# K S and Q K from one product: Q turned and the state side by side, moved as 112 columns

## The chip, the cores and the metric

The kernel runs on one core of a Trainium2 chip. The metric is device time in microseconds (us), from the start to the end of one execution. The engines are named as in the profile: PE is TensorE (PEld its weight loads), DVE is VectorE, ACT is ScalarE, POOL is GpSimd, SP issues most of the transfers.

## What is computed

A delta-rule attention over 4 batches, 8 heads, 768 steps and a head size of 48, and behind it a feed-forward block with a SiLU gate on 3072 tokens of width 384:

```python
k_n = k / (np.linalg.norm(k, axis=-1, keepdims=True) + 1e-06)
state = np.zeros((B, H, D, D))
for t in range(S):
    kt, vt, bt = k_n[:, :, t], v[:, :, t], beta[:, :, t, None]
    y[:, :, t] = einsum('bhd,bhde->bhe', q[:, :, t], state)
    v_old = einsum('bhde,bhd->bhe', state, kt)
    state = state + bt[..., None] * einsum('bhd,bhe->bhde', kt, vt - v_old)
x = y.transpose(0, 2, 1, 3).reshape(B * S, H * D)
g = x @ w_gate
out = (g * sigmoid(g) * (x @ w_val)) @ w_out       # d_ff = 1536
```

## The kernel before

The steps are cut into 12 chunks of C = 64. Within a chunk the recurrence becomes a few matrix products for each of the 32 pairs of batch and head. With K and Q the chunk's rows and S the state at its start: K K^T gives a triangular matrix that is inverted (for two chunks at a time, a group g), R = V - K S, U = inverse times R, the output is Y = Q S + P^T U, where P is K Q^T with a mask (`mask_q`) that keeps earlier steps only, and the new state is S + K^T U. K and Q are unnormalised; norms and beta go into the inverse and into V.

Pairs are numbered by `b` and `bp` (batch = 2 b + bp) and by `j` and `par` (head = 2 j + par). A product over all of them is 32 small matmuls that each use a quarter of PE's 128x128 array: two partition halves for `par` and two output halves. `every()` runs over them in an order that goes through the four quarters. In the profile each fp32 matmul counts as two instructions, so such a product shows as x64. Six banks of PSUM matter here: `px` and `py` are pairs of banks for all attention products in turn, `ffn0` to `ffn3` belong to the feed-forward block.

`turned(c, of_q)` writes the transposed K or Q of chunk c, up to c = 2 for Q (c = 5 for K) through PE and ACT, later by one transpose on DVE (L494), from blocks that SP loads. `gram_steps` (L521) multiplies K with K or with Q; for Q two DVE operations (L539) put the masked product into `p_sb`. `advance(c)` is the chunk's chain, cut by `yield` into four steps:

1. K S into `px` (L949), Q S into `py` (L937), R = V - K S on DVE (L959).
2. U = inverse times R into `px` (L987), copied out by ACT (L1008).
3. K^T U into `px` (L1089) and added to the state on DVE (L1098); P^T U onto Q S in `py` (L1077), copied out by ACT.
4. Y is transposed (L1150) into the feed-forward block's input.

From chunk 2 on the feed-forward block of chunk c is computed while chunk c + 1 advances. `gate_val_fast` runs three rounds of ten `product4` (L1259, four matmuls of 128 columns each, eight instructions in the profile); `output_fast` runs eight products of six matmuls with 192 columns (L1465). The order of all engines is written out by hand (`manual_schedule`): at fixed places of this stream, twice in a round and twice in an output, `point` issues one step of attention work, and `fill` then issues pieces of the inverse until a budget is used up. `spent` collects what DVE time the point has cost, and is taken from that budget. A point runs the next step of `advance` if it has begun, or else a step of `prep_step`: a join of the inverse (L898, L912), the second half of a `products` generator (the K K and Q K products of an upcoming chunk), or its first half (the turning). `may_advance(c)` lets a chunk begin once its masked P exists and its inverse is joined; `finish` forces what is left. The substitution in the inverse runs on POOL (L593, L599).

What PE issues in the rounds around a chunk's first steps is thus, in the profile's order: five `product4`, a point, six `product4` with the begin of the next round, a point, and so on.

Of the kernel before, what the change touches and what calls it, by code (L numbers as in the profile page):

```python
# [20 lines left out]
def kernel(  # L21
# [25 lines left out]
    nc = tc.nc  # L47

    B, H, S, D = q.shape
    NCH = S // C  # L50
    NJ = H // 2
    NB = B // 2
# [9 lines left out]
    const = ctx.enter_context(tc.tile_pool(name="const", bufs=1))  # L62
    work = ctx.enter_context(tc.tile_pool(name="work", bufs=2))
# [10 lines left out]
    def ps_pair(name, tag):  # L74

        return pairs_of_banks[tag]
# [84 lines left out]
    def load_blocks(of_q, c):  # L161

        x, _, t = blocks_of[of_q]
        x_v = x.rearrange("b (j par) s d -> par s b j d", par=2)
        t_v = t.rearrange("p bp h d -> p (bp h d)")
        t_v = t_v.rearrange("p (b j blk d) -> p b j blk d", b=B, j=NJ, blk=C // R)
        for par in range(2):
            for at in range(0, D, R):
                m = min(R, D - at)
                rows = slice(64 * par + at, 64 * par + at + R)  # L170
                for blk in range(C // R):
                    lo = c * C + R * blk
                    nc.sync.dma_start(
                        out=t_v[rows, :, :, blk, 0:m].rearrange("p b j d -> p (b j) d"),
                        in_=x_v[par, lo : lo + R, :, :, at : at + m].rearrange(
                            "s b j d -> s (b j) d"
                        ),
                    )
# [55 lines left out]
    for n, (name, lo) in enumerate(place_of):  # L234
        m = 2 * pieces[n][4]
# [85 lines left out]
    mask_q = const.tile([128, C], FP32, name="mask_q")  # L321
    nc.gpsimd.memset(mask_q, 1.0)
    for b in range(2):
        rows = mask_q[64 * b : 64 * b + 64]
        nc.gpsimd.affine_select(
            out=rows,
# [12 lines left out]
    p_places = [const.tile([128, 1024], FP32, name=f"p_sb{i}") for i in range(2)]  # L339
    spent, late_loads = [], []  # L340
# [2 lines left out]
        if late_loads:  # L343
            late_loads.pop(0)()

    state = const.tile([128, 2, NB, NJ, D], FP32, name="state")
    kt, qt, a_sb, a_of, p_sb, xts = {}, {}, {}, {}, {}, {}

    ORDER = ((0, 0), (1, 1), (0, 1), (1, 0))
# [1 line left out]
    def half_of(x):  # L351
        return slice(64 * x, 64 * x + 64)

    def head_of(x):
        return slice(64 * x, 64 * x + D)

    def every():
        for bp in range(NB):
            for j in range(NJ):
                for n, (par, b) in enumerate(ORDER):  # L360
                    yield bp, j, par, b, bp == 0 and j == 0
# [112 lines left out]
    def banks(name, tag):  # L474

        if type(tag) is int:
            return [ps_ffn([128, 512], name, tag + i) for i in range(2)]
        p = ps_pair(name, tag)
        return [p[:, 0], p[:, 1]]

    def turned(c, of_q, tag=None):

        if tag is None:
            tag = "py" if of_q else "px"
        x = qpad[c % QB] if of_q else kn_of(c)
        if of_q:
            xt = work.tile([128, NB * NJ * 2 * C], FP32, name="qt", bufs=1)
        else:
            xt = kt_of(c)
        if c >= blocks_of[of_q][1]:  # L490
            xt_v = xt.rearrange("p (b bp j i) -> p bp j b i", bp=NB, b=2, j=NJ)
            (qt if of_q else kt)[c] = xt_v
            blocks = blocks_of[of_q][2]
            nc.vector.transpose(xt, blocks.rearrange("p bp h d -> p (bp h d)"))  # L494
            spent.append(1.8)
            if c + 1 < NCH:
                late_loads.append(lambda: load_blocks(of_q, c + 1))
            return
        xt = xt.rearrange("p (bp j b i) -> p bp j b i", bp=NB, j=NJ, b=2)
        (qt if of_q else kt)[c] = xt  # L500
        p_t = banks("p_t", tag)
        for bp in range(NB):
            for j in range(NJ):
                at = slice(128 * j, 128 * j + 128)
                nc.tensor.transpose(p_t[bp][:, at], x[:, bp, 2 * j : 2 * j + 2], ident)
            if type(tag) is int:
                nc.scalar.copy(xt[:, bp].rearrange("p j b i -> p (j b i)"), p_t[bp])
        for bp in range(NB if type(tag) is not int else 0):
            nc.scalar.copy(xt[:, bp].rearrange("p j b i -> p (j b i)"), p_t[bp])
        if of_q and c + QB < Q_BLOCKS:  # L510
            load_q(c + QB)

# [42 lines left out]
    def gram(*args):  # L555
        for _ in gram_steps(*args):
            pass
# [212 lines left out]
    def recur(p, m=D):  # L770
        p = p[:, :, 0 : NB * NJ * m]
        return p.rearrange("p x (bp j d) -> p x bp j d", bp=NB, j=NJ)
# [148 lines left out]
        yield  # L921

    p_1 = []

    def advance(c):

# [5 lines left out]
        r = vin.pop(c)  # L932
        p_y = recur(ps_pair("p_y", "py"))

        def q_of_state():
            for bp, j, par, b, first in every():
                nc.tensor.matmul(  # L937
                    p_y[half_of(b ^ par), par, bp, j],
                    qt[c][head_of(par), bp, j, b],
                    state[head_of(par), b, bp, j],  # L940
                    start=first,
                    stop=False,
                    skip_group_check=True,
                )

        if c > 0:
            p_r = recur(ps_pair("p_r", "px"))
            for bp, j, par, b, first in every():
                nc.tensor.matmul(  # L949
                    p_r[half_of(b ^ par), par, bp, j],  # L950
                    kt[c][head_of(par), bp, j, b],
                    state[head_of(par), b, bp, j],
                    start=first,
                    stop=True,
                    skip_group_check=True,
                )
            if c > 1:
                q_of_state()
            nc.vector.tensor_tensor(out=r, in0=r, in1=p_r, op=ALU.subtract)  # L959
            if c == 1:  # L960
                next(p_1[0])
            spent.append(1.4)
            yield
# [18 lines left out]
        for bp, j, par, b, first in every():  # L982
            if c == 1:
                out = p_u_of[par ^ bp][half_of(b ^ bp), par, j]
            else:
                out = p_u_of[par][half_of(b), bp, j]
# [11 lines left out]
        elif c == 1:  # L998
            flat = v0.rearrange("p par bp j d -> p (par bp j d)")
            for bank in range(2):  # L1000
                p = p_u_of[bank].rearrange("p par j d -> p par (j d)")
# [24 lines left out]
        if c < 2:  # L1026
# [3 lines left out]
            for n in range(3):  # L1030
                if c > 0:
                    u = uu if n else v0
# [543 lines left out]
    def step(kind, fn, *args):  # L1576
        key = (kind, args or (1,))
        if key not in gens:
            gens[key] = [fn(*args), 0]
        if next(gens[key][0], None) != MORE:  # L1580
            gens[key][1] += 1

    def steps(kind, *args):
        return gens.get((kind, args), (None, 0))[1]
# [4 lines left out]
    def products(k_c, q_c):  # L1589

        if k_c is not None:
            turned(k_c, False)
        if q_c is not None:
            turned(q_c, True)
        yield
        if k_c is not None:
            gram(k_c, False, None, (nc.scalar.copy, nc.scalar.copy))
            if k_c % 2 == 1:
                fills.append((k_c // 2, invert(k_c // 2)))
        if q_c is not None:  # L1600
            gram(q_c, True)
        yield

# [2 lines left out]
    going = []  # L1606
# [10 lines left out]
    def may_advance(c):  # L1617
        g = c // 2
        due = {0: 0, 1: 2 + 2 * (c % 2)}.get(g, 2)
        return steps("advance", c) > 0 or (c in p_sb and steps("join", g) >= due)  # L1620

    def k_ready():

# [9 lines left out]
    def prep_step(c):  # L1633

        for g in range(1, c // 2 + 2):
            late = g == 1 and (
                hold or steps("join", g) >= 2 and steps("advance", 2) < 4
            )
            if g in inverted and steps("join", g) < (4 if g == 1 else 2) and not late:
                step("join", join if g > 1 else join_1, *((g,) if g > 1 else ()))  # L1640
                return True
        if going:
            next(going.pop())
            return True
        k_c, q_c = None, None
        if q_of and steps("advance", q_of[0] - 1) >= 3:
            q_c = q_of.pop(0)
        elif not (c > 0 and hold and not todo and k_ready()):
            return False
        if k_ready():  # L1650
            k_c = k_of.pop(0)
        gen = products(k_c, q_c)
        next(gen)
        going.append(gen)
        return True

    def point_and_fill(c, n, fill):
# [203 lines left out]
```

## Time and profile before

| | |
|---|---|
| median of 3 runs | 693.98 us (692.44 to 696.86) |
| profiled execution | 694.63 us, span of its instructions 692.9 us |
| granted TensorE clock | 0.996 |
| PE busy | 678.4 us, 98% |
| DVE busy | 410.8 us, 59% |
| ACT busy | 262.4 us, 38% |
| POOL busy | 194.4 us, 28% |
| L1259, x_ffn with the gate weights | 128.2 us, 840 instructions |
| L1465, wo_sb with h_f | 83.4 us, 480 instructions |

The span runs from the first to the last instruction of one execution; the execution's own time has 1.7 us more around it. Busy time is the union of an engine's instructions, so instructions that overlap in PE's pipeline count once, and the mean length of a PE instruction (275 ns in the first L1259 group) is latency, not the time after which the next can start. A group row has its count behind the x, then busy time in us and the mean of one in ns, then the idle time of the engine ahead of the group and what ended it.

### The profile page before, as it was taken

What the parts mean: (1) busy time and instruction counts of PE and PEld (TensorE: products, weight loads), DVE (VectorE), ACT (ScalarE), POOL (GpSimd) and SP (SyncE); (2) the same over time, 40 slices, a digit from 0 to 9 for tenths busy, and PEclk for the clock granted to TensorE, in tenths of its full rate; (3) what the DMA queues carried; (4) which work ended last, traced back from release to release, by engine and by line L of the source; (5) the groups of instructions that cost most, each with busy time, mean ns of one, the idle gap of its engine ahead of it and who ended that gap; (6) DMA issues with size and microseconds to landing.
All of it is one profiled execution on the core that took longest, in us unless ns stands there. A gap on an engine that the chain in (4) does not pass through costs nothing.

```text
span 692.9 us, 25453 instructions
## 1 busy us (share of the span) xinstructions
PE 678.4 (98%) x11272; PEld 631.5 (91%) x11272; DVE 410.8 (59%) x857; ACT 262.4 (38%) x554; POOL 194.4 (28%) x310
## 2 busy tenths in 40 slices
PE   8799999999999999999999999999999999999997
PEld 4587888656999999999999999999999999999997
DVE  6878679897657655547446457454565344333342
ACT  3785676214442532344233244233133242142230
POOL 5110031106882128820038820328800000000000
PEclk9999999999999999999999999999999999999999
DMA  9577925017550621464432373233253221221210
GB/s 132 141 185 178 271 67 163 7 35 175 127 111 13 117 79 39 104 121 78 92 74 70 70 138 70 60 82 71 66 120 70 56 63 47 56 62 46 70 46 23
DMA packets 143853, 62.29 MB, mean 90 GB/s; under 512 B 122976, under 2 KB 126048, under 8 KB 143744
## 3 DMA queue, kind: packets, MB, share of 16 engines
q1 hardware_dynamic: 141536, 60.19, 37.9%
q8 instruction: 88, 1.44, 0.9%
q10 hardware_dynamic: 2080, 0.39, 0.4%
q0 software_dynamic: 128, 0.10, 0.1%
q14 instruction: 21, 0.17, 0.1%
HBM read 53.58 MB, written 7.08 MB: 88 GB/s over the span
## 4 chain that ended last, share of the span: by engine, by line
PE 89%; DMA 4%; ACT 2%; SPq 2%; issue 1%; DVE 1%; POOL 0%; DVEq 0%; ACTq 0%
PE ffn L1259 43%; PE ffn L1465 20%; PE ffn L1355 6%; PE ffn L1382 4%; PE p_px L987 2%; PE p_px L949 2%; PE p_py L937 2%; PE p_py L521 1%; PE p_py L1077 1%; PE p_px L1089 1%; SPq L140 1%; DMA wo_sb<-in_moe_w_gate_dram 1%; DMA h_f<-in_moe_w_gate_dram 1%; PE p_px L521 1%; PE p_py L1150 1%
## 5 line engine op out<-in xcount | busy, mean ns | idle before, releaser
L1259 PE MATMUL ffn<-x_ffn,wg_sb 128*128 128x128 f32 x840 | 128.2, 275 | 0.0
L1259 PE MATMUL ffn<-x_ffn,wv_sb 128*128 128x128 f32 x840 | 128.1, 275 | 0.0
L1259 PEld LDWEIGHTS ffn<-x_ffn,wg_sb 128*128 128x128 f32 x840 | 111.1, 192 | 0.1
L1259 PEld LDWEIGHTS ffn<-x_ffn,wv_sb 128*128 128x128 f32 x840 | 110.7, 192 | 0.0
L1294 DVE TENSOR_TENSOR h_f<-sil,ffn 128x256 f32<-128x256 f32 x120 | 50.0, 418 | 78.6 <-ACT sil L1289 76.9
L1289 ACT ACTIVATE sil<-ffn 128x256 f32<-128x256 f32 x120 | 46.2, 385 | 132.4 <-PE ffn L1259 130.7
L1465 PE MATMUL ffn<-wo_sb,h_f 128*128 128x192 f32 x480 | 83.4, 327 | 0.0
L837 POOL TENSOR_TENSOR n_b<-mb,half 128x32 f32<-128x32 f32 x5 | 30.1, 6011 | 179.7 <-DVE mb L563 179.7
L1465 PEld LDWEIGHTS ffn<-wo_sb,h_f 128*128 128x128 f32 x480 | 78.1, 190 | 0.4
L1426 DVE TENSOR_TENSOR ffn<-ffn,p_sb 128x512 f32<-128x512 f32 x58 | 40.6, 699 | 63.5 <-ACT ffn L1315 62.2
L599 POOL TENSOR_TENSOR zb<-zb,tmp 128x31 f32<-128x31 f32 (+15 forms) x124 | 73.7, 595 | 9.7
L593 POOL TENSOR_TENSOR tmp<-zb,mb 128x31 f32<-128x31 f32 (+15 forms) x124 | 66.4, 535 | 16.0 <-DVE mb L580 6.6
L1259 PE MATMUL ffn<-x_t,h_f 128*128 128x128 f32 x480 | 61.1, 280 | 0.2 <-ACT ffn L1272 0.2
L1259 PEld LDWEIGHTS ffn<-x_t,h_f 128*128 128x128 f32 x480 | 56.2, 191 | 1.4 <-ACT ffn L1272 0.4
L1426 DVE TENSOR_TENSOR o_sb<-o_sb,ffn 128x192 f32<-128x192 f32 x49 | 17.3, 352 | 62.5 <-PE ffn L1465 60.9
L1272 ACT COPY ffn<-ffn 128x512 f32<-128x512 f32 x30 | 17.1, 571 | 63.8 <-PE ffn L1259 57.4
L1465 PE MATMUL ffn<-last_k,h_f 128*128 128x192 f32 x200 | 35.9, 327 | 0.0
L1423 DVE TENSOR_TENSOR h_f<-h_f,h_f 128x256 f32<-128x256 f32 x60 | 29.9, 507 | 9.1 <-PE ffn L1465 8.1
L1355 PE MATMUL ffn<-x_ffn,wg_sb 128*128 128x256 f32 x144 | 34.4, 385 | 0.2
L1355 PE MATMUL ffn<-x_ffn,wv_sb 128*128 128x256 f32 x144 | 33.9, 383 | 0.1
L1465 PEld LDWEIGHTS ffn<-last_k,h_f 128*128 128x128 f32 x200 | 32.9, 190 | 0.0
L1355 PEld LDWEIGHTS ffn<-x_ffn,wv_sb 128*128 128x128 f32 x144 | 26.9, 190 | 4.2 <-DVE h_f L1366 0.5
(306 smaller groups left out, 1096.1 us busy)
## 6 DMA issues: line engine op xcount, KB each, us to landing
h_f<-w_s SPq DMA_DIRECT2D x60, 256.0 KB, 2.8
p_sb<-w_s SPq DMA_DIRECT2D x27, 256.0 KB, 2.7
vin<-in_v_dram SPq DMA_DIRECT2D x48, 96.0 KB, 3.4
out_dram<-o_sb SPq DMA_DIRECT2D x48, 96.0 KB, 2.2
kn<-in_k_dram SPq DMA_DIRECT2D x20, 192.0 KB, 4.4
zt<-in_moe_w_out_dram SPq DMA_DIRECT2D x6, 384.0 KB, 3.6
qpad<-in_q_dram SPq DMA_DIRECT2D x36, 64.0 KB, 3.2
w_s<-h_f SPq DMA_DIRECT2D x7, 256.0 KB, 2.9
```

The source lines that it names most:

```text
L593: engine.tensor_tensor(out=t_v, in0=zb[:, 0 : j + 1, j : j + 1].to_broadcast([128, j + 1, m]), in1=mb[:, j : j + 1, j + 1 : R].to_broadcas ...
L599: engine.tensor_tensor(out=zb[:, 0 : j + 1, j + 1 : R], in0=zb[:, 0 : j + 1, j + 1 : R], in1=t_v, op=ALU.add,)
L837: nc.gpsimd.tensor_tensor(out=n, in0=mb.rearrange("p j i -> p (j i)")[:, 0 : R * R : R + 1], in1=half, op=ALU.pow,)
L1259: nc.tensor.matmul(p[:, u], w(u), moving, start=start and u == 0, stop=True, skip_group_check=True,)
L1272: nc.scalar.copy(p_y, p_x)
L1289: nc.scalar.activation(sil[:, n].rearrange("p (i n) -> p i n", i=2), p[:, 0:2], ACTF.Silu)
L1294: nc.vector.tensor_tensor(out=h_of(c, f, j), in0=sil[:, n].rearrange("p (i n) -> p i n", i=2), in1=p[:, 2:4], op=ALU.mult,)
L1355: nc.tensor.matmul(ps[name][:, i], w_sb[:, t, (f + i) * 128 : (f + i + 1) * 128], xts[c][:, t], start=(t == 0 and i == 0), stop=(t == KT - 1),
L1382: nc.tensor.matmul(p_o, hs[c, f - f % 2][:, f % 2, bp * 128 : (bp + 1) * 128], wo_sb[:, f], start=(f == 0), stop=(f == FT - 1),)
L1423: nc.vector.tensor_tensor(out=out, in0=a, in1=b, op=ALU.subtract)
L1426: nc.vector.tensor_tensor(out=out, in0=a, in1=b, op=ALU.add)
L1465: nc.tensor.matmul(p[x, part], a(f - f % 2)[:, f % 2], b(f), start=not begun and f == 0, stop=f == FH - 1, skip_group_check=True,)
```

## The change

Q turned and the state become parts of one tile `qs`: for each of the 16 index triples (b, bp, j) 64 columns of Q turned and then 48 columns of state. The turning of Q, its transpose on DVE and the state's update write into it with a stride of 112; the reads of the state and of Q elsewhere keep their form.

From chunk 3 on (`MERGED`) the Q K product in `gram` is no longer issued. In its place the first step of `advance` multiplies K with all 112 columns, `par` 0 into `px` and `par` 1 into `py`. DVE then takes R = V - K S from the last 48 columns in two operations, one for each `par`, and the masked P from the first 64 columns in three: one for `par` 0, and two for `par` 1, whose halves have to change places. Q S is issued at the start of the second step, ahead of U. The budget notes 3.4 for the first step in place of 1.4. `products` without K work ends after the turning, and a chunk may advance once Q is turned.

In the built program this removes 288 matmuls of 5710 on PE (32 in each of 9 chunks) and the order of PE's `product4` among themselves stays as it was. The wide product stands at the end of a round or of the output in eight chunks, in the middle of a round in chunk 5. From chunk 8 on the attention's steps stand a few points earlier.

```diff
-    state = const.tile([128, 2, NB, NJ, D], FP32, name="state")
+    qs = const.tile([128, 2 * NB * NJ, C + D], FP32, name="qs")
+    qs_v = qs.rearrange("p (b bp j) m -> p b bp j m", b=2, bp=NB)
+    q_t, state = qs[:, :, 0:C], qs_v[:, :, :, :, C : C + D]
...
+        late = c >= blocks_of[of_q][1]
         if of_q:
-            xt = work.tile([128, NB * NJ * 2 * C], FP32, name="qt", bufs=1)
+            xt_v = qs_v[:, :, :, :, 0:C].rearrange("p b bp j i -> p bp j b i")
...
+        if late:
+            blocks = blocks_of[of_q][2].rearrange("p bp h d -> p (bp h d)")
+            if of_q:
+                blocks = blocks.rearrange("p (u i) -> p u i", i=C)
+            nc.vector.transpose(q_t if of_q else kt_of(c), blocks)
...
     p_1 = []
+    MERGED = 3
...
-        if c > 0:
+        if c >= MERGED:
+            both = [
+                ps_pair("p_pr", tag)[:, :, 0 : NJ * (C + D)].rearrange(
+                    "p bp (j m) -> p bp j m", j=NJ
+                )
+                for tag in ("px", "py")
+            ]
+            for bp, j, par, b, _ in every():
+                nc.tensor.matmul(
+                    both[par][half_of(b ^ par), bp, j],
+                    kt[c][head_of(par), bp, j, b],
+                    qs_v[head_of(par), b, bp, j],
+                )
+            for par in range(2):
+                nc.vector.tensor_tensor(
+                    out=r[:, par],
+                    in0=r[:, par],
+                    in1=both[par][:, :, :, C : C + D],
+                    op=ALU.subtract,
+                )
+            p_sb[c] = p_places[1].rearrange(
+                "p (x bp j i) -> p x bp j i", x=2, bp=NB, j=NJ
+            )
+            for par, to, of in ((0, slice(0, 128), slice(0, 128)), (1, half_of(0), half_of(1)), (1, half_of(1), half_of(0))):
+                nc.vector.tensor_tensor(
+                    out=p_sb[c][to, par],
+                    in0=both[par][of, :, :, 0:C],
+                    in1=mask_q[of, None, None, :].to_broadcast(
+                        [of.stop - of.start, NB, NJ, C]
+                    ),
+                    op=ALU.mult,
+                )
+            spent.append(3.4)
+            yield
+            q_of_state()
+        elif c > 0:
...
-        if q_c is not None:
+        if q_c is not None and q_c < MERGED:
             gram(q_c, True)
...
-        return steps("advance", c) > 0 or (c in p_sb and steps("join", g) >= due)
+        return steps("advance", c) > 0 or ((c in p_sb or c >= MERGED and c in qt) and steps("join", g) >= due)
...
-        going.append(gen)
+        if k_c is not None or q_c < MERGED:
+            going.append(gen)
```

More of the change, by code (lines that the diff above doesn't have):

```diff
@@ L479, in banks @@
         return [p[:, 0], p[:, 1]]
+    P_T = "p (j b i) -> p j b i"
     def turned(c, of_q, tag=None):
@@ L485, in turned @@
         x = qpad[c % QB] if of_q else kn_of(c)
+        late = c >= blocks_of[of_q][1]
         if of_q:
-            xt = work.tile([128, NB * NJ * 2 * C], FP32, name="qt", bufs=1)
-        else:
[L489 to L494, printed above, removed]
+            xt_v = qs_v[:, :, :, :, 0:C].rearrange("p b bp j i -> p bp j b i")
+        elif late:
+            xt_v = kt_of(c).rearrange("p (b bp j i) -> p bp j b i", bp=NB, b=2, j=NJ)
+        else:
+            xt_v = kt_of(c).rearrange("p (bp j b i) -> p bp j b i", bp=NB, j=NJ, b=2)
+        (qt if of_q else kt)[c] = xt_v
+        if late:
[3 more added lines that the diff above has]
+            nc.vector.transpose(q_t if of_q else kt_of(c), blocks)
             spent.append(1.8)
@@ L498, in turned @@
             return
-        xt = xt.rearrange("p (bp j b i) -> p bp j b i", bp=NB, j=NJ, b=2)
-        (qt if of_q else kt)[c] = xt
         p_t = banks("p_t", tag)
@@ L506, in turned @@
             if type(tag) is int:
-                nc.scalar.copy(xt[:, bp].rearrange("p j b i -> p (j b i)"), p_t[bp])
+                nc.scalar.copy(xt_v[:, bp], p_t[bp].rearrange(P_T, j=NJ, b=2))
         for bp in range(NB if type(tag) is not int else 0):
-            nc.scalar.copy(xt[:, bp].rearrange("p j b i -> p (j b i)"), p_t[bp])
+            nc.scalar.copy(xt_v[:, bp], p_t[bp].rearrange(P_T, j=NJ, b=2))
         if of_q and c + QB < Q_BLOCKS:
```

## The prediction

> **What bounds the kernel now.** I read the page first, its engine table and its slices, then the waits of TensorE (PE) alone, then the timeline of PE through one chunk.
>
> ```profile
> span 692.9 us, 25453 instructions
> PE 678.4 (98%) x11272; PEld 631.5 (91%) x11272; DVE 410.8 (59%) x857; ACT 262.4 (38%) x554; POOL 194.4 (28%) x310
> PE   8799999999999999999999999999999999999997
> PEclk9999999999999999999999999999999999999999
> PE 89%; DMA 4%; ACT 2%; SPq 2%; issue 1%; DVE 1%; POOL 0%; DVEq 0%; ACTq 0%
> ```
>
> PE is busy in nine tenths or more of every slice from the fourth to the last but one, at full clock, and 89% of the chain that ended last is PE. A busy PE may still be a PE at less than its peak, so the second view matters more: asked for the waits of PE from 186 us (before the first chunk that the change touches) to the end, the trace answers with its heading alone, no wait. VectorE (DVE) between 171 and 693 us is at half load (third column):
>
> ```profile
> engine line waited for: us in total, times, longest us
> ...
> 171.00:693.00 522.00, 517.68 (x8498) 508.78 (x8483) 272.35 (x521) 171.74 (x365) 159.75 (x257) 1.00 0.34 75
> ```
>
> So from chunk 3 on the time is what PE's instructions cost, one behind the other. What the change is worth is a price list of PE, provided that the other engines still deliver in time. The prices stand in the timeline (start, length, engine, line; every fp32 matmul is two instructions, so 32 matmuls are x64, and a `product4` is x8):
>
> ```profile
> 447.62 1.16 PE L1259 MATMUL ffn<-x_ffn,p_sb 128*128 128x128 f32 x8
> ...
> 453.18 1.15 PE L949 MATMUL p_px<-state,kt 48*64 48x48 f32 x64
> 454.15 1.11 PE L937 MATMUL p_py<-state,qt 48*64 48x48 f32 x64
> 455.19 2.05 PE L1259 MATMUL ffn<-x_t,h_f 128*128 128x128 f32 x16
> ...
> 459.85 1.15 PE L987 MATMUL p_px<-vin,zt 64*64 64x48 f32 x64
> 460.93 1.16 PE L1259 MATMUL ffn<-x_ffn,p_sb 128*128 128x128 f32 x8
> ...
> 466.49 0.94 PE L1089 MATMUL p_px<-uu,kn 64*48 64x48 f32 x64
> 467.24 1.11 PE L1077 MATMUL p_py<-uu,p_sb 64*64 64x48 f32 x64
> 468.29 2.05 PE L1259 MATMUL ffn<-x_t,h_f 128*128 128x128 f32 x16
> ...
> 473.51 1.06 PE L1259 MATMUL ffn<-x_ffn,p_sb 128*128 128x128 f32 x8
> ...
> 477.98 2.12 PE L1465 MATMUL ffn<-wo_sb,h_f 128*128 128x192 f32 x12
> 479.93 2.11 PE L1465 MATMUL ffn<-last_k,h_f 128*128 128x192 f32 x12
> ...
> 483.92 1.16 PE L521 MATMUL p_py<-qt,kt 64*64 64x64 f32 x64
> 485.01 1.24 PE L1465 MATMUL ffn<-wo_sb,h_f 128*128 128x192 f32 x6
> ```
>
> The lengths contain pipeline latency; the starts give the cost. (1) Full-array work: from 473.51 to 477.98 five `product4`, 40 instructions of 128 columns, with nothing of the attention between: 4.47 us, 0.1117 each. With 192 columns it is 479.93 - 477.98 = 1.95 over 12, 0.1625 each. So 64 more moving columns cost 0.0508 us, 0.79 ns a column. (2) Small products sit as islands in this stream. 455.19 to 460.93 holds 40 such instructions (4.47) and the island of U (L987): 5.74 - 4.47 = 1.27 for one product. 447.62 to 455.19 holds 48 (5.36) and the island of K S and Q S: 7.57 - 5.36 = 2.21 for two. Hence a product of 64 instructions costs 0.94 and an island as such, getting in and out, 0.33. (3) Q K (L521) alone, 483.92 to 485.01, is 1.09 with the way out; with the entry it is an island of 1.27 too, although it moves 64 columns where U moves 48.
>
> **The change part by part.** *Removed:* the product Q K of chunks 3 to 11.
>
> ```profile
> L521 PE MATMUL p_py<-qt,kt 64*64 64x64 f32 x384 | 6.8, 219 | 0.0
> L521 PE MATMUL p_py<-qt,kn 64*64 64x64 f32 x128 | 2.3, 220 | 0.0
> L521 PE MATMUL p_py<-qt,last_k 64*64 64x64 f32 x64 | 1.1, 218 | 0.0
> L521 PE MATMUL p_px<-kt 64*64 64x64 f32 x256 | 4.6, 221 | 0.0
> L521 PE MATMUL p_px<-kn 64*64 64x64 f32 x128 | 2.3, 221 | 0.0
> ```
>
> In the stretch from 171 us on these are 576 instructions into p_py, 9 products of 64, and 384 of K K into p_px, 6 products. Six of the nine Q K share an island with K K; in chunks 9, 10 and 11 there is no K K left, Q K stands alone, and its island goes with it. Gain: 9 x 0.94 = 8.5, and 3 x 0.33 = 1.0.
>
> *Widened:* K S moves 112 columns in place of 48, in the same 64 instructions with the same K as weights. No row has 112 columns in a quarter of the array, so I bound it. Sixteen groups of four quarter-array instructions make 0.94, 58 ns a group; by the full-array line of (1) a single instruction of 64 columns would take 0.1117 - 64 x 0.00079 = 0.061. Four quarters side by side thus cost what one full instruction of that width costs, and for 112 columns this gives 0.099 a group, 1.58 a product: 0.64 more than now. Lower bound: no dearer than now, 0.94, as 48 and 64 columns cost the same. Upper bound: the wide streams of two quarters take turns, 2 x 1.58 = 3.17. I take 1.58, because the rows of 64, 128 and 192 columns lie on its line. Nine times 0.64 is 5.8.
>
> Why 48 and 64 columns cost the same: L1089, with 48 weight columns (64*48), runs 466.49 to 467.24, 0.75; L949, with 64 (48*64) and the same 48 moving, takes 453.18 to 454.15, 0.97. It was the weights that set K S's pace, and there lies the point of merging: one set of weights is loaded where there were two.
>
> A rule speaks against this. The Trainium skill, page "TensorE: Matmul & The Clock Gate", section "Part 3: Packing small matmuls — row/col tiling", says that a weight load overlaps running matmuls only if it goes to another row group. By it a group would be weights plus stream in sequence, the wide product would cost about 2.5, and the sum would end slower than before. The trace disagrees so far: at 58 ns for 64 columns, there is no room for the two behind each other.
>
> *Moved:* Q S (L937) goes from K S's island into that of U, one `point` later; an island of one and one of two become an island of one and one of two. Zero for PE. Before Q S can write `py`, the masks must have read it, a new wait.
>
> *DVE.* One subtraction of 128x768 and two masks of 128x512 become two subtractions of 128x384 and three masks, one of 128 rows and two of 64, in a row right behind the wide product:
>
> ```profile
> L539 DVE TENSOR_TENSOR p_sb<-p_py,mask_q 128x512 f32<-128x512 f32 x22 | 14.2, 686 | 7.8 <-PE p_py L521 7.8
> L959 DVE TENSOR_TENSOR vin<-vin,p_px 128x768 f32<-128x768 f32 x11 | 10.5, 954 | 10.3 <-PE p_px L949 9.8 <-ACT last_h L278 0.3
> L1426 DVE TENSOR_TENSOR uu<-v,ffn 128x384 f32<-128x384 f32 x6 | 3.3, 555 | 3.2 <-PE ffn L1016 3.2
> L383 DVE TENSOR_REDUCE n_t<-ksq 64x8 f32<-64x384 f32 x4 | 2.2, 547 | 0.1
> L383 DVE TENSOR_REDUCE n_t<-ksq 128x8 f32<-128x384 f32 x2 | 1.0, 524 | 0.0
> L494 DVE STREAM_TRANSPOSE qt<-qpad 128x1024 f32<-128x1024 f32 x9 | 10.9, 1214 | 0.0
> L779 DVE STREAM_TRANSPOSE zt<-zb 128x1024 f32<-128x1024 f32 x1 | 2.2, 2241 | 0.0
> ```
>
> Half the rows save no time (547 against 524), so a mask of 64 rows is 0.686. Together 2 x 0.555 + 3 x 0.686 = 3.17, against 0.954 + 1.37 = 2.33 before: 0.84 more a chunk, 7.6 over nine, on an engine with 250 us free. The turning of Q writes rows of 64 with gaps: between 1.21 (contiguous) and 2.24 (the scattered L779). I take 1.21, as its runs are whole chunks; at 2.24 it is 1.0 more, covered likewise.
>
> What covers the 3.17: in the built order the wide product stands at the end of a round or of the previous chunk's output in eight chunks, and five `product4` follow before Q S; in chunk 5 it stands in mid-round and six follow. Five are 459.85 - 455.19 = 4.66 with entry. That leaves about 1.4. Queued behind the masks on DVE is the addition into p_y, whose cost and place before show here, with the group rows of what comes after it:
>
> ```profile
> 454.40 0.95 DVE L959 TENSOR_TENSOR vin<-vin,p_px 128x768 f32<-128x768 f32 x1 [1.16 <-PE p_px L949]
> 457.93 0.70 DVE L1426 TENSOR_TENSOR ffn<-ffn,p_sb 128x512 f32<-128x512 f32 x1 [2.58 <-ACT ffn L1315]
> ...
> L1294 DVE TENSOR_TENSOR h_f<-sil,ffn 128x256 f32<-128x256 f32 x120 | 50.0, 418 | 78.6 <-ACT sil L1289 76.9
> L1423 DVE TENSOR_TENSOR h_f<-h_f,h_f 128x256 f32<-128x256 f32 x60 | 29.9, 507 | 9.1 <-PE ffn L1465 8.1
> ```
>
> DVE idles 2.58 us ahead of that addition, so the 3.17 - 0.95 = 2.2 us more fall into idle time. PE needs the sum only behind the island of Q S and U, 4.66 + 2.21 = 6.9 us after the wide product; it would be there at 3.17 + 0.70, about 4. In chunk 5 the products with sil and the sums of h are behind the masks, at worst until 3.17 + 3 x 0.42 + 3 x 0.51 = 6.0; PE fills their banks again behind that island, six `product4` (5.36) and 2.2 us later. So zero for PE; without the cover each us of lateness is a us of PE, nine times.
>
> *Around it:* the q-only step of `prep_step` is gone and the masked steps leave the fill less room (3.4 in place of 1.4), so inverses and joins shift. In the built order the transposes that need GpSimd's substitution stand some 50 us of PE work behind its start, as before (the substitutions take 73.7 + 66.4 us for four, 35 each):
>
> ```profile
> L599 POOL TENSOR_TENSOR zb<-zb,tmp 128x31 f32<-128x31 f32 (+15 forms) x124 | 73.7, 595 | 9.7
> L593 POOL TENSOR_TENSOR tmp<-zb,mb 128x31 f32<-128x31 f32 (+15 forms) x124 | 66.4, 535 | 16.0 <-DVE mb L580 6.6
> ```
>
> The same transfers go out on SP, those of Q for chunks 9 to 11 up to 12 us earlier, on DMA engines 34% busy. Zero.
>
> **The sum.** -8.5 - 1.0 + 5.8 = -3.7 us. The profiled execution took 694.63 (span 692.9 and 1.7 around it): 690.9. It lies 0.65 above the median of the three runs, 693.98; so 690.3 for a median, from which the rivals are reckoned too.
>
> **The rivals.** (a) *The wide product is free*, bound as now by its weights: -9.5, 684.5. For it: 48 against 64 columns. Against it: 128 against 192 columns, where columns are paid. (b) *The wide product does not share the array*: its weights are no longer hidden behind the stream, 58 + 99 ns a group, 2.51 a product, +1.57 - 0.94 a chunk; with the islands +4.7, 698.7; at the upper bound of 3.17 it is +10.6, 704.6. It turns into a loss from 1.99 a product, 124 ns a group. This is also what the skill's rule, above, comes to. For it: no row shows columns well above the weights' width in a quarter; against it: 58 ns at 64 columns. (c) *The masks are late*: the burst exceeds its 4.66 and Q S waits. For it: DVE works in order, and a fill of 1.2 to 2.4 us may stand ahead of the burst. Against it: 1.4 us of slack and half an engine idle. Half a us of wait in each chunk is +4.5 and leaves 694.8; 1.2 in each, 701.1.
>
> **How the numbers follow.** The forecast itself, 689 to 692.5, gets 0.68, (a) 0.10, (b) 0.10, (c) 0.12. Within 1% (687.0 to 700.9, about what a measurement of this kernel can tell from no change) lie the forecast, half of (b) and half of (c): 0.79. Faster by over 1% is (a), 0.10; slower is the other half of (b) and (c), 0.11. The range runs from 685.5, leaving out most of (a), to 698, leaving out (b) and the worse half of (c).
>
> **What would show it.** Right: 64 instructions of 112 columns a chunk, from their first start to the next `product4` some 1.7 us; PE still without waits; islands of L521 into p_py gone from 186 us on; DVE with five operations of 3.2 us in all behind each. Wrong: a wait of PE at L937 on DVE or a gap there, or a start-to-start of the wide groups of four far from 0.099 us.

## The result and the profile after

The changed kernel takes 691.5 us (median of 9 runs, 690.57 to 692.67) against 695.01 (9 runs, 692.44 to 696.86) before it beside it: ratio 0.995, interval 0.9935 to 0.9966. That is 3.5 us less, within 1%, where 690.3 and 3.7 us less were forecast. The profiled execution took 690.57 us. In its profile the lines of the code have other numbers: `product4` is L1301 (was L1259), the output L1507 (L1465), the wide product L961, Q S L944, K K and Q K L527 (L521), the state L1131, P U L1119, the subtraction of K S L967, the masks L977, the addition into p_y L1468.

The page of after, its head, the slices of PE and the chain:

```profile
span 688.5 us, 24321 instructions
PE 674.0 (98%) x10696; PEld 627.2 (91%) x10696; DVE 416.4 (60%) x875; ACT 261.6 (38%) x554; POOL 192.6 (28%) x310
PE   8899999999999999999999999999999999999997
PE 91%; ACT 2%; DMA 2%; SPq 2%; issue 1%; DVE 1%; POOL 0%; DVEq 0%; ACTq 0%; POOLq 0%
```

576 matmul instructions are gone, as announced, and PE is still the bound. But where PE had no wait from 186 us to the end before, it now has three:

```profile
engine line waited for: us in total, times, longest us
PE ffn L1301 <- DVE qs L1140: 1.1, 1, 1.1
PE ffn L1301 <- ACT ffn L1357: 0.3, 2, 0.2
```

The wide product itself, from its first start to the next `product4` (timeline of PE: start, length):

```profile
440.31 0.31 PE L961 MATMUL p_px<-qs,kt 48*64 48x112 f32 x1
...
440.46 0.26 PE L961 MATMUL p_px<-qs,kt 48*64 48x112 f32 x1
...
441.80 0.26 PE L961 MATMUL p_px<-qs,kt 48*64 48x112 f32 x1
...
442.01 0.38 PE L1301 MATMUL ffn<-x_t,h_f 128*128 128x128 f32 x1
```

It takes 1.70 us, the 1.7 foretold. From the second group of four (440.46) to the last (441.80) are 14 steps: 0.0957 us a group. It is the same in all nine chunks. And the burst on DVE behind it (timeline of DVE; the number in brackets is its idle time before):

```profile
442.13 0.56 DVE L967 TENSOR_TENSOR vin<-vin,p_px 128x384 f32<-128x384 f32 x1 [1.15 <-PE p_py L961]
442.60 0.55 DVE L967 TENSOR_TENSOR vin<-vin,p_py 128x384 f32<-128x384 f32 x1
443.06 0.68 DVE L977 TENSOR_TENSOR p_sb<-p_px,mask_q 128x512 f32<-128x512 f32 x1
443.78 1.39 DVE L977 TENSOR_TENSOR p_sb<-p_py,mask_q 64x512 f32<-64x512 f32 x2
```

From 442.13 to the end of the masks at 445.17 it is 3.04 us, as neighbours overlap a little; Q S never waits for it.

To see where the time went, each trace is cut at the output transposes of chunk 2 (L1150 before, L1192 after), ahead of the first changed island. What lies behind this cut, up to PE's last instruction, is called the late stretch; it repeats closely from one execution to the next (three executions with the products of before: 519.34, 519.29, 519.29 us). Its two ends, before and then after:

```profile
169.51 0.87 PE L1150 MATMUL p_py<-ident,y 128*128 128x128 f32 x6
...
686.74 2.11 PE L1465 MATMUL ffn<-wo_sb,h_f 128*128 128x192 f32 x12
```

```profile
167.12 0.88 PE L1192 MATMUL p_py<-ident,y 128*128 128x128 f32 x6
...
682.83 1.63 PE L1507 MATMUL ffn<-wo_sb,h_f 128*128 128x192 f32 x9
```

What lies ahead of the cut does not repeat: the cut came at 167.12 and 170.30 us in two executions of after, at 169.51 before and at 167.47 and 169.34 with the layout alone. Late stretch: before 519.34, after 517.34. So 2.0 of the profile's 4.1 us lie in the changed chunks; 2.4 lie ahead of the cut, in a stretch whose products the change does not touch, and what an execution takes outside its span is 0.3 longer after (2.07 against 1.73).

PE's waits break the 2.0 down. From output to output the chunks without a wait are 0.31 to 0.35 us shorter where K K is still issued and 0.67 shorter in chunks 9 to 11 (chunks 8 and 9 taken together, as the transposes of chunk 8 now stand 88 instructions of `product4` earlier); six times the first and three times the second make 3.9. Chunk 4 is 0.13 longer and chunk 5 1.22 longer, which makes waits that cost 0.44 in chunk 4, and 0.44 and 1.1 in chunk 5. (The view of the waits counts only PE's idle time, 0.17 of each 0.44; the cost is counted from start to start.) Together that is the 1.9 by which the 3.9 exceed the 2.0.

### The profile page after: what moved, and what is told of

Read it like the earlier page. It is cut to its first block, busy times and chain, and to the rows that moved or that the text cites. A ratio compares the mean times of both kernels' runs of the same rounds, so it can differ in the third digit from the quotient of the medians.

```text
span 688.5 us, 24321 instructions
## 1 busy us (share of the span) xinstructions
PE 674.0 (98%) x10696; PEld 627.2 (91%) x10696; DVE 416.4 (60%) x875; ACT 261.6 (38%) x554; POOL 192.6 (28%) x310
## 4 chain that ended last, share of the span: by engine, by line
PE 91%; ACT 2%; DMA 2%; SPq 2%; issue 1%; DVE 1%; POOL 0%; DVEq 0%; ACTq 0%; POOLq 0%
PE ffn L1301 43%; PE ffn L1507 20%; PE ffn L1397 9%; PE ffn L1424 4%; PE p_px L961 2%; PE p_py L944 2%; PE p_px L1029 2%; PE p_py L1119 1%; PE p_px L1131 1%; SPq L140 1%; DMA h_f<-in_moe_w_gate_dram 1%; PE p_px L527 1%; PE p_py L1192 1%; PE ffn L1058 1%; PE p_px L904 1%
## 5 line engine op out<-in xcount | busy, mean ns | idle before, releaser
L1301 PE MATMUL ffn<-x_ffn,wg_sb 128*128 128x128 f32 x840 | 128.4, 275 | 0.6 <-ACT ffn L1357 0.3
L1301 PE MATMUL ffn<-x_ffn,wv_sb 128*128 128x128 f32 x840 | 128.1, 275 | 0.0
L1301 PEld LDWEIGHTS ffn<-x_ffn,wg_sb 128*128 128x128 f32 x840 | 111.1, 192 | 1.0 <-ACT ffn L1357 0.7
L1301 PEld LDWEIGHTS ffn<-x_ffn,wv_sb 128*128 128x128 f32 x840 | 110.7, 192 | 0.0
L1507 PE MATMUL ffn<-wo_sb,h_f 128*128 128x192 f32 x480 | 83.4, 327 | 0.0
L1507 PEld LDWEIGHTS ffn<-wo_sb,h_f 128*128 128x128 f32 x480 | 78.1, 190 | 0.3
L599 POOL TENSOR_TENSOR tmp<-zb,mb 128x31 f32<-128x31 f32 (+15 forms) x124 | 68.9, 556 | 16.9 <-DVE mb L586 7.5
L605 POOL TENSOR_TENSOR zb<-zb,tmp 128x31 f32<-128x31 f32 (+15 forms) x124 | 69.6, 561 | 9.7
L1468 DVE TENSOR_TENSOR ffn<-ffn,p_sb 128x512 f32<-128x512 f32 x58 | 40.3, 695 | 48.7 <-ACT ffn L1357 47.3
L1301 PE MATMUL ffn<-x_t,h_f 128*128 128x128 f32 x480 | 61.0, 280 | 0.2 <-ACT ffn L1314 0.2
L1301 PEld LDWEIGHTS ffn<-x_t,h_f 128*128 128x128 f32 x480 | 56.3, 191 | 2.1 <-ACT ffn L1314 0.4
L1468 DVE TENSOR_TENSOR o_sb<-o_sb,ffn 128x192 f32<-128x192 f32 x49 | 17.2, 352 | 63.6 <-PE ffn L1507 60.9
L1465 DVE TENSOR_TENSOR h_f<-h_f,h_f 128x256 f32<-128x256 f32 x60 | 30.2, 509 | 11.4 <-PE ffn L1507 10.2
L1507 PE MATMUL ffn<-last_k,h_f 128*128 128x192 f32 x200 | 36.0, 327 | 0.0
L1507 PEld LDWEIGHTS ffn<-last_k,h_f 128*128 128x128 f32 x200 | 32.9, 190 | 0.1
L1397 PEld LDWEIGHTS ffn<-x_ffn,wg_sb 128*128 128x128 f32 x144 | 26.5, 190 | 4.8 <-DVE wg_sb L309 0.8
```

The lines of the kernel that those rows point to most:

```text
L599: engine.tensor_tensor(out=t_v, in0=zb[:, 0 : j + 1, j : j + 1].to_broadcast([128, j + 1, m]), in1=mb[:, j : j + 1, j + 1 : R].to_broadcas ...
L605: engine.tensor_tensor(out=zb[:, 0 : j + 1, j + 1 : R], in0=zb[:, 0 : j + 1, j + 1 : R], in1=t_v, op=ALU.add,)
L1301: nc.tensor.matmul(p[:, u], w(u), moving, start=start and u == 0, stop=True, skip_group_check=True,)
L1397: nc.tensor.matmul(ps[name][:, i], w_sb[:, t, (f + i) * 128 : (f + i + 1) * 128], xts[c][:, t], start=(t == 0 and i == 0), stop=(t == KT - 1),
L1465: nc.vector.tensor_tensor(out=out, in0=a, in1=b, op=ALU.subtract)
L1468: nc.vector.tensor_tensor(out=out, in0=a, in1=b, op=ALU.add)
```

## The experiments

**1. The layout alone, and the merging of three chunks.** Does the early stretch gain, and what is a merged chunk worth without neighbours?

```diff
-    MERGED = 3
+    MERGED = 12     # layout alone
+    MERGED = 9      # chunks 9 to 11 alone
```

> Turned Q and the state lie side by side, but no product is merged: every product, mask and wait is that of before. Theory (the gain comes from the tensor engine's price of the removed and added matmuls in chunks 3 to 11): the layout gives nothing, 695.0 us as before, within 0.6. Rival (the early stretch gives part of it: in the profile of after the tensor engine is 1.9 us ahead before the first changed island; a place in the memory or the strided copies of turned Q could do that): 693.1 us here, and the profile is ahead by 1.5 to 2 us at 175 us.

> Only chunks 9 to 11 take the wide product; there Q K stood in an island of its own, with no K K beside it. Theory (per merged chunk 0.94 of Q K and, where no K K shares the island, 0.33 of entering and leaving go, and 0.60 to 0.64 of the wider product comes): 3 x 0.65 = 2.0 us less than before, so 693.0, and no tensor engine wait of 0.44 or 1.1 us, since K K keeps Q K behind it in chunks 3 to 8. Rival (the gain is in the joint islands and the order of chunks 3 to 8): under 1 us, 694.2 or more.

The layout alone: 694.22 us against 694.8 before (ratio 0.9992, 0.9971 to 1.0014); late stretch 519.29; no wait of PE from 186 us on. The cut came at 167.5 us in its profile, as early as in after, and the median did not follow: the 2.4 us that after's profile is ahead at the cut belong to that execution and not to the change. Chunks 9 to 11 alone: 692.28 us (0.9968, 0.9947 to 0.9989), late stretch 517.25, no wait of PE. 519.29 - 517.25 = 2.04, 0.68 a chunk: 0.94 + 0.33 less and 0.60 more. Merging three chunks thus brought in the trace all that merging nine did (517.34): chunks 3 to 8 gained 1.9 and gave 1.9 back in waits.

**2. The price of a column.** Narrower and wider moving data in the same instructions.

```diff
-                    qs_v[head_of(par), b, bp, j],
+                    qs_v[head_of(par), b, bp, j, 0:C],      # 64 columns
...
-                    in1=both[par][:, :, :, C : C + D],
+                    in1=both[par][:, :, :, 0:D],
...
-    qs = const.tile([128, 2 * NB * NJ, C + D], FP32, name="qs")
+    qs = const.tile([128, 2 * NB * NJ, C + D + 12], FP32, name="qs")   # 124 columns
```

The narrow kernel leaves out K S, and DVE subtracts columns of K Q in its place, so it is a probe of the price only.

> As after, but the merged product moves turned Q alone, 64 columns; K S is not computed, and the subtraction takes the first 48 columns of K Q in its place, so every other instruction, mask and wait stays. Theory (a group of four goes at 58 ns with 64 columns, as K K, and at 95.4 ns with 112 in the profile of after, so a column above 64 costs 0.78 ns): 16 groups x 37 ns x 9 products = 5.4 us less than after, 686.1. Rival (the group of four does not share the array, or the product is hidden behind something): a group stays at 90 ns or more, 690 to 691.5.

> As after, with 12 columns of zeros behind each block of turned Q and state, moved along: 124 columns in place of 112. Theory (0.78 ns a column): 104.8 ns a group, 0.15 us a product, 1.35 us more than after, 692.9. Rival (the price goes in steps, and 112 pays what 128 pays): 95 ns a group as with 112, 691.5.

The windows of one product each, with 64 columns and with 124 (in the latter kernel lines stand one further on):

```profile
437.92 0.27 PE L961 MATMUL p_px<-qs,kt 48*64 48x64 f32 x1
...
439.01 0.38 PE L1301 MATMUL ffn<-x_t,h_f 128*128 128x128 f32 x1
```

```profile
493.03 0.32 PE L962 MATMUL p_px<-qs,kt 48*64 48x124 f32 x1
...
494.88 0.38 PE L1302 MATMUL ffn<-x_t,h_f 128*128 128x128 f32 x1
```

1.09, 1.70 and 1.85 us for 64, 112 and 124 columns; groups of four every 58, 95.7 and 105.6 ns. A column above 64 costs 0.79 ns a group, then 0.83: the price follows a line and shows no steps. The medians are 686.93 us (0.9892, 0.9856 to 0.9928) and 694.93 (1.0004, 0.9978 to 1.003); late stretches 511.58 and 518.41. The narrow one is 5.76 less than after (5.43 by the product, 0.32 by a shorter wait in chunk 5), the wide one 1.07 more (1.43 by the product, a wait shorter by 0.56 and a new one of 0.18). The wide one's median is 3.4 above that of after, measured apart from it, where its late stretch accounts for 1.1; the rest stays open. The Trainium skill, "TensorE: Matmul & The Clock Gate", "Part 3: Packing small matmuls — row/col tiling", has weight loads overlap running matmuls only in another row group; at 95.7 ns for 112 columns, on the line through the other widths, no weight load stands exposed, and rival (b) falls.

**3. Does the cover of the masks count?** Each mask is issued twice.

```diff
+              for _ in range(2):
                 nc.vector.tensor_tensor(
                     out=p_sb[c][to, par],
```

> As after, with each of the three mask sums issued twice: the burst behind the wide product becomes 3.16 + 3 x 0.686 = 5.2 us on the vector engine. Theory (it is hidden by two groups of ffn products, 4.66 us, and then Q S must wait for bank p_py): 0.55 us of waiting ahead of Q S in eight chunks, 4.4 us more than after, 695.9. Rival (Q S has more slack than that, or the burst is hidden whatever its length): no wait at Q S, 691.5.

```profile
PE p_py L944 <- DVE p_sb L978: 5.3, 8, 0.7
```

```profile
201.58 0.56 DVE L967 TENSOR_TENSOR vin<-vin,p_px 128x384 f32<-128x384 f32 x1 [0.92 <-PE p_py L961]
...
203.96 2.84 DVE L978 TENSOR_TENSOR p_sb<-p_py,mask_q 64x512 f32<-64x512 f32 x4
```

These are the waits of PE, and the timeline of DVE in one chunk. The masks end at 206.80 and PE starts Q S at 206.85; so it goes in eight chunks, 0.7 us late each, and the late stretch is 523.45, 6.1 more than after. Chunk 5, with six `product4` in between, has no such wait. Q S would have stood at 206.12 (the wide product ends at 201.46, and 4.66 behind it); the burst of after, without the three added masks of 0.686, would have ended 2.06 earlier, and that leaves 1.4 us of slack, as predicted. The median is 700.88 us (1.0079, 1.0049 to 1.0109), 3 us more than the late stretch explains; in its profile the cut came at 173.4.

**4. The two waits on ACT.** What stands before the copy that they wait for? ACT in chunk 4, before and then after:

```profile
227.68 0.59 ACT L547 COPY a_sb<-p_px 128x512 f32<-128x512 f32 x1 [0.55 <-PE p_px L521]
228.30 0.74 ACT L550 COPY a_sb<-p_px 32x256 f32<-32x256 f32 x2
229.05 0.59 ACT L547 COPY a_sb<-p_px 128x512 f32<-128x512 f32 x1
229.67 0.74 ACT L550 COPY a_sb<-p_px 32x256 f32<-32x256 f32 x2
230.43 0.59 ACT L1312 COPY p_sb<-ffn 128x512 f32<-128x512 f32 x1
230.91 0.59 ACT L1315 COPY ffn<-ffn 128x512 f32<-128x512 f32 x1
```

```profile
224.97 0.59 ACT L553 COPY a_sb<-p_px 128x512 f32<-128x512 f32 x1 [0.55 <-PE p_px L527]
...
228.20 0.59 ACT L1357 COPY ffn<-ffn 128x512 f32<-128x512 f32 x1
```

They are the same six copies of K K, with the same 3.2 us from the first to the ffn copy. PE's products around it, before and then after:

```profile
231.70 0.61 PE L1259 MATMUL ffn<-x_ffn,wv_sb 128*128 128x128 f32 x4
232.15 0.61 PE L1259 MATMUL ffn<-x_ffn,wg_sb 128*128 128x128 f32 x4
```

```profile
228.06 0.61 PE L1301 MATMUL ffn<-x_ffn,wv_sb 128*128 128x128 f32 x4
228.84 0.71 PE L1301 MATMUL ffn<-x_ffn,wg_sb 128*128 128x128 f32 x4 [0.17 <-ACT ffn L1357]
```

Before, the ffn copy ended at 231.50, 0.65 us ahead of the product that needs its bank. After, it ends at 228.79, and the product, due at 228.51, starts at 228.84: 0.33 late, and its four instructions take 0.10 more than their neighbours, together the 0.44. Q K used to run behind K K in the same island, and its 0.93 us were the cover of ACT's copies. In the other four chunks with a K K product PE does not wait. Two ways to relieve the copies:

```diff
-            gram(k_c, False, None, (nc.scalar.copy, nc.scalar.copy))
+            gram(k_c, False)                       # the two wide copies on DVE
...
+        if not of_q and c >= 4:                # or: joined over both banks, ahead of the loop of six
+            both = a_sb[c // 2][:, c % 2]
+            nc.scalar.copy(
+                both.rearrange("p (x h) i -> p x (h i)", x=2),
+                p_both,
+            )
+            for hi in (QUADS[0][0], QUADS[2][0]):
+                nc.scalar.copy(
+                    both[hi, :, R:C].rearrange("p (x h) i -> p x h i", x=2),
+                    p_both[hi].rearrange("p x (h i) -> p x h i", i=C)[:, :, :, 0:R],
+                )
+            yield
+            return
```

> As after, but the two wide copies of each K K go to the vector engine, the four narrow ones stay on the scalar engine. Theory (the two waits of 0.44 us at product4 in the profile of after come from six copies of K K, 2.7 us, that stand on the scalar engine ahead of the copies that free the ffn banks, since Q K no longer runs behind K K): both waits go, 0.9 us less than after, 690.6. Rival (the bank is late for another reason, or the vector engine's burst and its own sums become late): waits of the same size stay or move to sums of the vector engine, 691.5 or more.

> As after, but the copies of K K from chunk 4 on stay on the scalar engine and are three in place of six: one of 1024 columns over both banks and two narrow ones over both banks, by the rows of after some 1.05 + 2 x 0.59 = 2.2 us in place of 2.66. Theory (the two waits of 0.44 at product4 come from the scalar engine's copies of K K ahead of the ffn copies): both fall to 0.1 or less, 0.7 to 0.9 us less than after, 690.7. Rival (the ffn copies are late for another reason): both waits stay, 691.5.

> The joined copies of K K, unchanged, beside after on the same chip. Theory (the two waits of 0.44 us are gone, nothing else changes): 0.9 us less than after, the late stretch 515.8 to 516.5 us. Rival (the difference is within the spread of the early stretch): no difference that the medians show, 0.3 us or less, with the late stretch shorter all the same.

On DVE it went wrong: 694.26 us (0.999, 0.9963 to 1.0017, against before), late stretch 520.24, and the wait in chunk 4 became 2.57 us from start to start. DVE and ACT there:

```profile
227.12 1.54 DVE L880 STREAM_TRANSPOSE z<-zt 32x256 f32<-32x256 f32 x4
228.68 0.69 DVE L553 COPY a_sb<-p_px 128x512 f32<-128x512 f32 x1
230.18 0.69 DVE L553 COPY a_sb<-p_px 128x512 f32<-128x512 f32 x1 [0.80 <-ACT a_sb L556]
```

```profile
229.41 0.74 ACT L556 COPY a_sb<-p_px 32x256 f32<-32x256 f32 x2 [3.17 <-DVE a_sb L553]
230.90 0.74 ACT L556 COPY a_sb<-p_px 32x256 f32<-32x256 f32 x2 [0.76 <-DVE a_sb L553]
231.66 0.58 ACT L1354 COPY p_sb<-ffn 128x512 f32<-128x512 f32 x1
```

The transposes of the join stood ahead of the copy on DVE, ACT's narrow copies waited for the wide ones, and the ffn copies stood behind them. I had named DVE's load and not its order there. The wait cost more than itself: behind it, up to 237.1 us, sixteen matmuls of `product4` start 0.213 us apart in place of 0.112, and the trace shows the granted clock at half from 233.63 to 237.04. That is 1.6 us more, which together with the longer waits on ACT (2.1 and 0.2) and without the 1.1 of chunk 5 makes the 2.9 by which the late stretch is longer than that of after. Joined on ACT it went as expected:

```profile
225.58 1.01 ACT L544 COPY a_sb<-p_px 128x1024 f32<-128x1024 f32 x1 [0.55 <-PE p_px L528]
226.62 1.17 ACT L549 COPY a_sb<-p_px 32x512 f32<-32x512 f32 x2
227.81 0.59 ACT L1368 COPY p_sb<-ffn 128x512 f32<-128x512 f32 x1
228.30 0.59 ACT L1371 COPY ffn<-ffn 128x512 f32<-128x512 f32 x1
```

From the first copy to the ffn copy it is 2.7 us in place of 3.2; both waits of 0.44 are gone in both executions, late stretches 515.72 and 515.81. The medians are 691.18 and 691.49 us (0.9939, 0.9916 to 0.9961, and 0.9948, 0.9926 to 0.9971, against before). That is 0.3 below after each time (691.5, measured apart from it, and 691.85 beside it): it beats before, and in the late stretch after too, but the medians do not separate it from after.

**5. The wait of 1.1 us in chunk 5.** It is put down to a DVE addition that had ended at 300.23:

```profile
298.81 0.41 PE L1131 MATMUL p_px<-uu,kn 64*48 64x48 f32 x20
299.03 1.11 PE L1119 MATMUL p_py<-uu,p_sb 64*64 64x48 f32 x64
301.20 0.57 PE L1301 MATMUL ffn<-x_ffn,p_sb 128*128 128x128 f32 x3 [1.05 <-DVE qs L1140]
```

Nothing else in the trace ended just ahead of 301.20. What PE also needs is its instructions, and they arrive as transfers during the run (queues of before, then after: packets, MB, share):

```profile
q8 instruction: 88, 1.44, 0.9%
```

```profile
q8 instruction: 84, 1.38, 0.8%
```

11272 matmuls and as many weight loads over 88 packets are 256 instructions a packet, and 10696 over 84 are 255. The packets lie all over the span. In the feed-forward stream 128 matmuls, with their weight loads 256 instructions, take 14.3 us (128 x 0.1117); the islands of state and P U use up as many in 2. The change takes away 1152 instructions and so shifts where packets end. The test: shift by half a packet, at two places.

```diff
-        unread(5)
+        p = ps_pair("p_t", "px")[:, 0]
+        for _ in range(35):                                     # at the start, where PE waits for K
+            nc.tensor.matmul(p[0:R, 0:4], half, half[:, 0:4])
+        unread(2)
...
-        for bp, j, par, b, _ in every():
+        for bp, j, par, b, _ in list(every()) * (2 if c == 4 and not of_q else 1):   # K K of chunk 4
```

> As after, but at the very start, where the tensor engine waits for K, 70 matmul instructions of 4 columns and 4 of 512 stand in place of 10 of 512: with their weight loads 128 instructions more, half a 16 KB packet of instructions. Everything behind stays. Theory (the wait of 1.1 us behind the P U island of chunk 5 is a late packet of instructions: two islands in a row use up 256 instructions in 2 us, and removing the matmuls of Q K has shifted where packets end): with the packets' ends shifted by half, this wait is gone or stands at another place. Rival (a semaphore: a late bank or tile): the same wait of 1.1 us stays at the same matmul. The time: 691.5, less 0 to 1.1.

> As after, with the K K product of chunk 4 issued twice into the same bank, at 187 us: 64 matmuls and 64 weight loads more, 128 instructions, half a packet, in an island that is there anyway; nothing ahead of it changes. Theory (the wait behind the P U island of chunk 5 is a late packet of instructions): it is 0.1 us or less here, as in the run with the early shift, and a wait for nothing that the profile shows may stand in another run of small products; the late stretch is 517.4 + 0.94 - up to 1.1. Rival (the wait belongs to the semaphore or the loads at that place): 0.3 to 1.1 us stay at the same matmul.

In both the wait at P U is gone (in the first one, 306.63 follows P U at once):

```profile
305.58 1.11 PE L1119 MATMUL p_py<-uu,p_sb 64*64 64x48 f32 x64
306.63 0.60 PE L1301 MATMUL ffn<-x_ffn,p_sb 128*128 128x128 f32 x3
```

And in both a new one stands in the middle of one and the same product, a join of chunk 6, the first kernel and then the second (which has one more, of 0.2 us, in the join of chunk 4):

```profile
343.68 1.17 PE L918 MATMUL p_py<-t,z 32*32 32x32 f32 x115
346.23 0.32 PE L918 MATMUL p_py<-t,z 32*32 32x32 f32 x13 [1.38 <-issue]
```

```profile
347.41 1.17 PE L918 MATMUL p_py<-t,z 32*32 32x32 f32 x115
349.72 0.32 PE L918 MATMUL p_py<-t,z 32*32 32x32 f32 x13 [1.14 <-issue]
```

115 of 128 matmuls run, 13 come over 1 us later, with nothing for them to wait for. That the place moves with the phase of the packets, to the same matmul from two different insertions, and that it can lie inside a product, speaks for late instructions and against a semaphore or a load at P U. Its length is not fixed by the phase: with the phase of after it cost 1.1, 0.9, 0.8, 0.5, 0.35, 0.33 and 0.4 us in seven executions (after twice, the narrow, the wide, the masks, the joined copies twice). With the copies on DVE, after a longer wait earlier in the chunk, it was none.

The records of queue q8 in the traces settle it. In all seven executions PE goes on 1.3 to 1.6 us after one and the same packet, the 40th, has landed (in the first, 299.64 and 301.20); the two new waits end as far behind the 45th (344.79 and 346.23; 348.21 and 349.72). And in all traces of this case, from 23 us on, each of the 57 waits of over 0.15 us that are put down to "issue" ends 1.2 to 1.65 us after a packet has landed, where packets come some 8 us apart. So the wait is PE running out of instructions, and its length depends on when the packet comes; why it comes when it does stays open.

The times went against me: 697.58 us (1.004, 1.0023 to 1.0057) and 699.53 (1.0062, 1.004 to 1.0084), 6 and 8 more than after. The late stretches are 517.94 and 517.97, only 0.6 more; the cuts came at 173.59 and 177.05. The doubled K K stands at 82 us and not at 187 as I had written. In the early stretch of the first kernel the waits for nothing that the profile shows add up to 6.5 us, against 2.8 in after, and in the second to 8.2; but those of the second lie partly ahead of 82 us, where its instructions are those of after. Both traces also show the granted clock at half for 6.8 us of the early stretch, against 3.4 in after. So it is seen where this loss lies, late packets above all, and not why these packets come later.

**6. After and the layout again, on one chip.**

> After, unchanged, beside the layout alone on the same chip. Theory (from the y transposes of chunk 2 to the end the trace of after is 2.0 us shorter than that of before and of the layout alone, and up to 0.8 more where the wait in chunk 5 is short; the rest of the 3.5 us between the medians is spread of the early stretch): 2.0 to 2.9 us less than the layout alone, the late stretch 516.6 to 517.4 us. Rival (the early stretch of after is steadily shorter): 3.5 us less or more than the layout alone, and the y transposes of chunk 2 start before those of the layout alone by over 1 us.

> The layout alone, unchanged, beside after on the same chip. Theory: as before within 0.6 us, the late stretch 519.3 us. Rival (the layout gives something in the early stretch): 1 us or more less than before.

After 691.85 us (0.9942, 0.9918 to 0.9965), the layout alone 694.51 (0.9995, 0.9979 to 1.0011), before 694.75. Late stretches 517.13 and 519.29, 2.16 apart; the medians 2.7 apart, as are the earlier ones (694.22 - 691.5), which were not measured side by side. The cut of this after came at 170.30, later than the layout's. In the late stretch the change is worth 2.0 and 2.2 us as measured, and would be worth 2.7 with the shortest wait seen in chunk 5; the median of the first comparison, 3.5, has an interval of 2.4 to 4.5.

## Why the prediction was right, and where not

- *PE's price list, right.* Q K went at 0.94 and three islands at 0.33, and the wide product is 0.60 dearer where 0.64 was estimated (experiments 1 and 2). The sum by PE was -3.7 and is -3.9.
- *The wide product shares the array, right.* 0.0957 us a group against 0.099; rivals (a) and (b) fall with the line through 64, 112 and 124 columns.
- *Masks at zero, right, and for the reason given.* Slack 1.4 us, shown by using it up (experiment 3); rival (c) needs a burst 1.4 longer.
- *The smaller terms of DVE, right.* The strided turning of Q was put at 1.21 and took 1.215; a mask of half the rows was put at 0.686 and took 0.688.
- *"PE still without waits", wrong.* The failing step is the part on what lies around the change: I followed who covers DVE's new work and not what the removed Q K had been covering. ACT's copies lost 0.93 us of cover with 0.65 to spare, which gave 0.44 in each of two chunks, 0.9 in all. Joining the copies takes both waits away (experiment 4). Nor did I count that 1152 instructions less move the ends of PE's instruction packets: 0.33 to 1.1 us in chunk 5 (experiment 5).
- *The size.* -3.9 + 0.9 + 0.3 to 1.1 gives 1.9 to 2.7 less, and the late stretches of after show 2.0 and 2.2; with the shortest wait seen in chunk 5 it would be 2.7. The medians show 3.5 and 2.9, which is this plus the spread of the early stretch. That they came so close to the 3.7 is in part luck: in the traces PE gave back about half of what it gained.

## What to carry to other kernels

Before a product is taken off the bound engine, ask what ran in its shadow: here six copies of another engine lost their cover, and about half of the gain went into waits. When medians of two kernels differ by less than the early stretch varies, cut the traces at a mark ahead of the change and compare what follows. The price of merging products with the same weights is that of the added moving columns; here it was below the price of the product that it replaced, and merging paid best where that product was an island of its own.

## What the runs showed of the hardware

PE's instructions come in packets of 256 during the run (22544 over 88 packets). In runs of small matmuls (128 in one to two us) a packet can come too late: PE then stood for 0.2 to 1.8 us, inside a product as well as between two, and went on 1.2 to 1.65 us after the packet had landed; 128 instructions more moved the place. After PE had stood for 2.3 us, the granted clock was at half for 3.4 us (experiment 4). Four quarter-array instructions side by side, each with 64 weight columns, cost 58 ns at 48 and at 64 moving columns and 0.79 to 0.83 ns for each column more, up to 124. On ACT one copy of 1024 columns over two banks took 1.01 us where two of 512 took 1.18.
